# GFNet mixing and a SoLU block on one core: entry 0 stays in one SBUF buffer, and the output weights are converted in steps 0 to 3

## The chip, the cores and the metric

The kernel runs on one core of one Trainium2 chip. A core has five engines with instruction queues of their own: TensorE (PE, matrix products into PSUM), VectorE (DVE), ScalarE (ACT), GpSimd (POOL) and SyncE (SP, which issues DMAs here). Each engine works through its own queue in order; semaphores hold an instruction until what it needs is there. DMAs are issued from the queues of SP, ACT and POOL. The metric is the device time of one execution in microseconds.

## The reference

The first half is a global filter over the sequence, for 8 batch entries of 3136 positions by 256 channels; the second half is a SoLU block over the 25088 rows that come out.

```python
X = np.fft.rfft(x, axis=1)                       # (8, 3136, 256)
Y = X * (filt_r + 1j * filt_i)[None]
y = np.fft.irfft(Y, n=3136, axis=1)              # -> (25088, 256)

h = y @ w_in                                     # 256 -> 1024
sm = softmax(h)                                  # with 1e-9 in the denominator
solu = h * sm
ln = (solu - mean) / np.sqrt(var + 1e-6) * g_ln
out = ln @ w_out                                 # 1024 -> 256
```

The weights w_in and w_out arrive as 8-byte floats; the kernel reads them as pairs of 32-bit words and converts them to fp32 with integer operations on DVE.

## The kernel before, in words

**The transform.** 3136 = 49 x 64. Two ends of the 64 are folded onto each other, so one entry is held as 98 rows (2 x 49) by 32 places by 256 channels. Four products make the filter: *pa* over the 49 (98 rows in, 100 rows out: 25 frequencies s times 4 parts a), *pb* over the 64 (one pair of frequencies at a time, with tables *de*), the product with the filter on DVE (*multiply*: four products of 128x512 and two adds), *pc* back over the 64 (*inverse*), and *py* back over the 49. Between pa and pb the roles of partitions and free places change: pa leaves (s, a) on the partitions and the place m free; pb wants (a, m) on the partitions and s free. The same turn is wanted, the other way, between pc and py. The kernel before makes both turns through DRAM: `store_first` writes pa's result to d1, `fetch` reads it back in the other order; `store` writes pc's result to d2 and `fetch_first_back` reads it.

**The opening** handles entry 0 alone, before anything else can run: its eight pieces of x (four places each) into one tile `rows_x`, pa per piece with a copy by ACT (L240), the trip over d1, seven units of pb, multiply and pc (start, multiply, inverse in one loop; `idle` products keep PE busy in gaps), the trip over d2, and py into y (`back`, L409, copies on ACT at L412). Beside it stand the loads of the filters and tables (`load_tables`, eight filter DMAs and one table each for three groups), the transposes of the tables (`tables_back`, L497), the loads of the weights' words (`begin`) and their conversion (`convert`, `load_float64`): four blocks of w_in and four of w_out, of 128x512 each. Blocks of w_in are multiplied by powers with a negative sign, and use ACT for one product and POOL for another and the add; those of w_out use DVE for all but the add. Blocks 0 and 1 are converted while d1 is written, 2 and 3 while d2 is written and read, the four of w_out beside py and the first products. `weight_sums` makes four differences of w_in blocks for the seven-product scheme below. The remaining jobs of the opening are six pieces of x of entry 1 into free room in y (`fetch_second`, L476) and four stores of the filters in their loaded order to f_dram (L624).

**The steps.** After that, 196 blocks of 128 rows pass through `step(k)`, two blocks (a pair j) per two steps, in an order written out by hand. The products h = y @ w_in of a pair take seven products m1 to m7 of 128x512 on sums of halves (`product`, L759; the sums s on POOL in `pair_sums`), brought together by ACT (`keep`, L769) and DVE (`finish`, L783 and L780, which also keep a running maximum). Then ACT takes the exponential, DVE multiplies (`normalize`, L805), DVE transposes 32x32 blocks (`turn`, L823), SP regroups by DMA (`regroup`, L840), POOL makes sums (L738) and PE multiplies by w_out (`project`, L895) from step LAG = 9 on. So step 9 is the first that needs w_out. `prepare_w_out` makes w_out ready in seven parts, all called at the end of step 0: scale by g_ln (16 operations, L696) and set the ones; the mean over rows on PE (`ps_mean`, L704) with a copy on ACT; four subtractions of the mean (L709); four differences of blocks (L157).

Entry 1's transform runs inside steps 0 to 22 (the table PLAN gives the step of each pa, pb and back), its pa products in steps 0 and 1 (L238), its pb from step 4 on. `early`, `middle`, `late`, `loads`, `first_parts` and so on are lists of such jobs, called at fixed places in `step`. The order inside one engine's queue is the order in which the program issues; nothing is moved at run time.

Of the kernel before, what the change touches and what calls it, by code (L numbers as in the profile page):

```python
# [17 lines left out]
P = 128  # L18
# [34 lines left out]
def dft_tables():  # L53
# [19 lines left out]
    for a, part, sign in ((0, 0, 1), (1, 1, -1), (2, 1, 1), (3, 0, 1)):  # L73
# [19 lines left out]
    return wf.reshape(NR, NK).astype(f32), wq.reshape(P, 2, 64).astype(f32), \  # L93
        wi.reshape(NK, NR).astype(f32), wb.reshape(P, N1).astype(f32), de.astype(f32)
# [3 lines left out]
def kernel(  # L98
# [11 lines left out]
    wf_host, wq_host, wi_host, wb_host, de_host = dft_tables()  # L110
    wf_dram = nc.inline_tensor(wf_host, name="wf_tbl").ap()
    wq_dram = nc.inline_tensor(wq_host, name="wq_tbl").ap()
# [26 lines left out]
    wi_t = consts.tile([NK, NR], FP32, name="wi_t")  # L139
# [56 lines left out]
    class Spectrum:  # L196
# [144 lines left out]
        def inverse(self, i, pss):  # L341
            de, prods = self.des.pop(i), self.prods.pop(i)
            for r in range(2):
                for u in range(self.shape(i)[0]):
                    rows = slice(NQ * u, NQ * u + NQ)
                    self.product(i, pss[u][NQ * r:NQ * r + NQ], lambda v: de[rows, v, 1, r, :],
                                 prods[r][rows])
            self.gs[i] = self.buffer(i, "g", [P, 4, C])
            for u in range(self.shape(i)[0]):
                w = self.shape(i)[1]  # L350
                nc.scalar.copy(out=self.gs[i][:, u:2 * w:2, :], in_=pss[u][:, 0:w, :])
# [6 lines left out]

    def fetch_first_back(ch):
        d = d2[0].rearrange("s (a n) c -> (s a) n c", a=4)  # L360
        for rows in (slice(0, NK - 4), slice(NK - 4, NK)):
            for n in ([0, 1] if ch == 0 else [ch] if ch > 1 else []):
                nc.sync.dma_start(out=t4s[0, n][rows], in_=d[rows, NCH * n:NCH * n + NCH, :])
# [52 lines left out]
    with ExitStack() as st:  # L416
        fpool = pool("fp", 1, stack=st)
        pools = {name: pool(name + "0", bufs, stack=st)
                 for name, bufs in (("r", 1), ("t2", 1), ("p", 2), ("g", 4))}
        wpool = pool("wp", 5, stack=st)  # L420
        ps_h = pool("ps_h", 3, PSUM, stack=st)

        def load_words(src, n):
            raw = wpool.tile([P, 512, 2], I32, name=f"raw_{n}", tag="raw")
            nc.gpsimd.dma_start(
                out=raw.rearrange("p (k d) w -> p k d w", d=src.shape[-2]) if len(src.shape) == 4 else raw,
                in_=src)
            return raw

        def load_float64(dst, raw, negate, share, add=nc.gpsimd.tensor_tensor):  # L430
# [3 lines left out]
            power = wpool.tile([P, 512], I32, name="power", tag="power", bufs=2)  # L434
# [7 lines left out]
            if negate:  # L442
                ts(out=power, in0=power, scalar1=255.0, scalar2=None, op0=ALU.min)
                ts(out=power, in0=power, scalar1=23, scalar2=-2 ** 31, op0=ALU.logical_shift_left,
                   op1=ALU.bitwise_or)
            else:
                ts(out=power, in0=power, scalar1=255.0, scalar2=2.0 ** 23, op0=ALU.min, op1=ALU.mult)
# [7 lines left out]
            if share:  # L455
                nc.scalar.mul(rest, lo, 2.0 ** -44)
                nc.gpsimd.tensor_tensor(out=rest, in0=rest, in1=power.bitcast(FP32), op=ALU.mult)
            else:
                stt(out=rest, in0=lo, scalar=2.0 ** -44, in1=power.bitcast(FP32), op0=ALU.mult,
                    op1=ALU.mult)  # L460
            add(out=dst, in0=dst, in1=rest, op=ALU.add)
# [45 lines left out]
        for h in range(2):  # L507
            for half in range(2):
                weights.append((w_out_sb[:, (0, 6, 1, 2)[2 * h + half]].rearrange("p k d -> p (k d)"),
                                w_out_words[512 * h:512 * h + 512, P * half:P * half + P].rearrange(  # L510
                                    "(k p) d w -> p k d w", p=P)))
# [11 lines left out]
        def begin(j):  # L523
            raws[j] = load_words(weights[j][1], j)
# [4 lines left out]

        rows_x = pools["r"].tile([P, NH, C], FP32, name="x_0", tag="r")  # L530
# [7 lines left out]

        st.enter_context(tc.manual_schedule())
        nc.sync.dma_start(out=wf_t, in_=wf_dram)  # L540
# [4 lines left out]
        fetch_x(0, 0, NH, N1 - 1, 1, nc.sync.dma_start)  # L545
        for i in range(pieces):
            if i:
                fetch_x(0, NCH * i, NCH, 0, N1 - 1, nc.sync.dma_start)
            fetch_x(1, NCH * i, NCH, 0, N1, nc.gpsimd.dma_start)
            if i in (4, 7):  # L550
                begin(i // 7)
        load_tables(0, 4, nc.gpsimd.dma_start)
        load_tables(4, 4, nc.gpsimd.dma_start)
        for i in range(pieces):
            sp.xs[i] = rows_x[:, NCH * i:NCH * i + NCH]

            sp.first(i, (0, 1), ps_h.tile([P, 2, 512], FP32, name=f"pa_0_{i}", tag="h"),
                     nc.scalar.copy, sp.xs[i][0:NK])
            sp.store_first(i, 0, lambda out, in_: by_16((nc.scalar.dma_start, nc.sync.dma_start), out, in_))
# [10 lines left out]
        idle_row(5, "idle")  # L570

        def convert(j):
            load_float64(weights[j][0], raws.pop(j), negate=j < 4, share=j < 4,
                         add=(nc.vector if j == 7 else nc.gpsimd).tensor_tensor)

        for j in range(2):
            convert(j)

        def start(i):
            sp.fetch_filter(i)  # L580
# [5 lines left out]
        sp.fetch(0, nc.sync.dma_start)  # L586
        for i in range(1, units - 2):
            sp.fetch(i, nc.sync.dma_start, spare_piece(i - 1))
            if i == 3:
                load_tables(8, NP - 8, nc.sync.dma_start)  # L590
        for i in range(2):
            start(i)
            tables_back(4 * i, 4)
        for i in range(units):
# [4 lines left out]
            sp.multiply(i, 0, nc.vector.tensor_tensor)  # L599
# [3 lines left out]
            sp.inverse(i, pss)  # L603
            sp.store(i, nc.scalar.dma_start)
            if i == 0:
                nc.gpsimd.dma_start(out=wi_t, in_=wi_dram)
                nc.gpsimd.dma_start(out=wq_t, in_=wq_dram)
                nc.gpsimd.dma_start(out=wb_t[:, 0:N1], in_=wb_dram)
                nc.gpsimd.dma_start(out=g_sb, in_=moe_g_ln.rearrange("(k p) -> p k", p=P))
            elif i == 1:  # L610
                for last_one in (units - 2, units - 1):
                    sp.fetch(last_one, nc.gpsimd.dma_start, spare_piece(last_one - 1))
            for j in {2: (2,), 3: (3, 4), 4: (5,), 5: (6,)}.get(i, ()):
                begin(j)
        idle_row(14, "idler")
        rows_t4 = pools["r"].tile([P, NH, C], FP32, name="t4_0", tag="r")
        for ch in range(pieces):
            t4s[0, ch] = rows_t4[0:NK, NCH * ch:NCH * ch + NCH]
        for ch in range(pieces):
            fetch_first_back(ch)  # L620
# [556 lines left out]
```

## Time and profile before

| | us |
|---|---|
| three runs | 1606.48, 1591.15, 1596.14 |
| median | 1596.14 |
| the profiled execution | 1601.33 |
| its span in the trace | 1599.6 |

| engine | busy us | share of the span |
|---|---|---|
| PE, products | 1551.8 | 97% |
| DVE | 1250.7 | 78% |
| POOL | 1169.7 | 73% |
| ACT | 921.4 | 58% |

The profile is of one execution, with times from the start of its span. A line of the timeline gives the start, the duration, the engine, the line in the kernel, the operation, what it writes and reads, its shape and how many were merged; in brackets stands how long the engine was idle before it and what ended that. "Busy" of PE is modelled from pipelined products, so a busy PE need not be at its peak. The granted clock is that which PE got, as a share of full speed. Some moments of the opening: the first pa starts at 10.6, the first pb at 42.1, the first py at 81.4, the first product of step 0 at 95.7; the DMAs move 267 GB/s on average from 0 to 100 us.

### The profile page before, as it was taken

The page shows a single profiled execution, that of the slowest core. Times are in us where ns is not written, and L with a number is a line of the kernel's source. Part 1 is how long each engine was busy: PE and PEld are TensorE (multiplying, and loading weights), DVE is VectorE, ACT ScalarE, POOL GpSimd, SP SyncE. Part 2 cuts the span into 40 slices and gives each one's busy share as a digit, 9 for nine tenths or more (in the row PEclk, how much of TensorE's full clock was granted, in tenths as well). Part 3 has the DMA queues.
Part 4 walks back from the last instruction along what each step waited for, and adds up shares of the span by engine and source line. Part 5 has one row for each costly group of instructions (what it writes and reads, how often), then busy time and mean ns, then how long its engine had stood idle before and what let it go on. Part 6 is the DMA issues. An engine that isn't in the chain of part 4 may idle for free.

```text
span 1599.6 us, 36769 instructions
## 1 busy us (share of the span) xinstructions
PE 1551.8 (97%) x12828; PEld 1058.8 (66%) x12828; DVE 1250.7 (78%) x2248; ACT 921.4 (58%) x1874; POOL 1169.7 (73%) x1371
## 2 busy tenths in 40 slices
PE   5998999999999999999999999999999999999997
PEld 1463566666666676677666677667766777777777
DVE  1887878897987788876988789887888777777673
ACT  2246555656665656666565655666565656666663
POOL 5546886789677868796779867797766766676765
PEclk8999999999999999999999999999999999999999
DMA  9989878786987589766886679766784444343434
GB/s 266 290 282 269 247 215 236 215 217 181 255 241 222 155 229 256 211 183 178 221 231 202 166 193 251 204 189 179 215 224 132 126 133 122 103 113 94 116 105 116
DMA packets 343802, 311.13 MB, mean 195 GB/s; under 512 B 27834, under 2 KB 310099, under 8 KB 343619
## 3 DMA queue, kind: packets, MB, share of 16 engines
q1 hardware_dynamic: 271476, 170.45, 40.6%
q0 software_dynamic: 33744, 98.81, 21.0%
q10 hardware_dynamic: 38400, 39.53, 8.2%
q8 instruction: 104, 1.70, 0.5%
q14 instruction: 78, 0.64, 0.1%
HBM read 124.51 MB, written 81.40 MB: 129 GB/s over the span
## 4 chain that ended last, share of the span: by engine, by line
PE 84%; DMA 9%; DVE 2%; POOL 1%; issue 1%; SPq 1%; ACT 0%; DVEq 0%; POOLq 0%; ACTq 0%
PE m L759 35%; PE o L895 34%; DMA solu_t<-turn 4%; PE py L386 4%; PE pc L313 3%; PE pb L313 3%; PE pa L281 2%; DMA x<-in_x_dram 2%; DMA f<-in_filt_r_dram 1%; SPq L840 1%; PE idler L563 1%; PE pa L238 1%; PE py L409 1%; DMA out_dram<-ot 1%; POOL u L738 1%
## 5 line engine op out<-in xcount | busy, mean ns | idle before, releaser
L895 PEld LDWEIGHTS o<-w_out_sb,solu_t 128*128 128x128 f32 x3136 | 381.5, 192 | 50.2 <-issue 43.6
L895 PE MATMUL o<-w_out_sb,solu_t 128*128 128x128 f32 x3136 | 400.9, 276 | 3.6 <-DVE ot L915 2.9
L759 PE MATMUL m<-w_in_sb,s 128*128 128x512 f32 x784 | 399.0, 610 | 2.7 <-ACT h L769 1.8
L895 PEld LDWEIGHTS o<-w_out_sb,u 128*128 128x128 f32 x2352 | 307.1, 192 | 138.9 <-issue 106.0
L895 PE MATMUL o<-w_out_sb,u 128*128 128x128 f32 x2352 | 310.6, 275 | 2.5 <-POOL u L738 1.8
L759 PE MATMUL m<-w_in_sb,y 128*128 128x512 f32 x588 | 307.6, 606 | 1.5 <-DVE h L780 1.1
L805 DVE SCALAR_TENSOR_TENSOR h<-e,h 128x1024 f32<-128x1024 f32 x196 | 304.1, 1551 | 0.1
L769 ACT COPY h<-m 128x512 f32<-128x512 f32 x294 | 173.2, 589 | 206.5 <-PE m L759 187.0
L911 ACT ACTIVATE ot<-o,rs_t 128x128 f32<-128x128 f32 x392 | 143.6, 368 | 245.2 <-PE o L895 243.8
L738 POOL TENSOR_TENSOR u<-solu_t 128x512 f32<-128x512 f32 x98 | 135.5, 1383 | 195.6 <-DMA solu_t<-turn 133.6
L783 DVE CUSTOM_DVE_ANT_0 h<-m,h 128x512 f32<-128x512 f32 x196 | 134.2, 685 | 176.8 <-ACT h L769 103.0
L813 ACT ACTIVATE h<-h,nmu 128x1024 f32<-128x1024 f32 x196 | 225.0, 1148 | 52.0 <-DVE turn L823 51.8
L823 DVE STREAM_TRANSPOSE turn<-h 128x1024 f32<-128x1024 f32 x196 | 243.1, 1240 | 3.2
L793 ACT ACTIVATE e<-h,nmax 128x1024 f32<-128x1024 f32 x196 | 225.4, 1150 | 7.9 <-DVE h L805 6.5
L738 POOL TENSOR_TENSOR u<-solu_t,u 128x512 f32<-128x512 f32 x98 | 137.7, 1405 | 95.8 <-PE o L895 95.5
L759 PEld LDWEIGHTS m<-w_in_sb,s 128*128 128x128 f32 x784 | 128.1, 191 | 89.5 <-issue 68.9
L915 DVE SCALAR_TENSOR_TENSOR ot<-o,rs_t,ot 128x128 f32<-128x128 f32 x299 | 103.7, 347 | 98.8 <-ACT ot L911 59.0
L738 POOL TENSOR_TENSOR u<-u,solu_t 128x512 f32<-128x512 f32 x98 | 159.1, 1624 | 15.5 <-PE o L895 6.4
L759 PEld LDWEIGHTS m<-w_in_sb,y 128*128 128x128 f32 x588 | 96.6, 191 | 96.7 <-issue 46.6
L738 POOL TENSOR_TENSOR solu_t<-solu_t,solu_t 128x512 f32<-128x512 f32 x98 | 153.9, 1571 | 0.9
L738 POOL TENSOR_TENSOR s<-y 128x128 f32<-128x128 f32 x196 | 99.8, 509 | 0.5
L386 PEld LDWEIGHTS py<-wb_t,t 50*64 50x64 f32 x3584 | 57.6, 134 | 42.9 <-issue 18.7
(126 smaller groups left out, 1969.1 us busy)
## 6 DMA issues: line engine op xcount, KB each, us to landing
solu_t<-turn SPq DMA_DIRECT2D x780, 128.0 KB
out_dram<-ot SPq DMA_DIRECT2D x196, 128.0 KB
t<-d POOLq DMA_DIRECT2D x112, 200.0 KB, 7.0
d<-x POOLq DMA_DIRECT2D x100, 200.0 KB, 5.3
f<-f_dram POOLq DMA_DIRECT2D x39, 512.0 KB, 8.1
t<-d ACTq DMA_DIRECT2D x37, 512.0 KB
d<-g POOLq DMA_DIRECT2D x36, 512.0 KB, 5.1
x<-in_x_dram SPq DMA_DIRECT2D x112, 98.0 KB
```

The costliest lines, as they stand in the source:

```text
L386: nc.tensor.matmul(out=views[g][64 * h:64 * h + 64, cb, i, :], lhsT=t4[rows, i, c0:c0 + 64], rhs=wb_t[rows, 0:N1], start=True, stop=True)
L738: nc.gpsimd.tensor_tensor(out=out, in0=in0, in1=in1, op=op)
L759: nc.tensor.matmul(out=ms[j, bank], lhsT=lhsT, rhs=w_in_sb[:, w, :], start=m in (1, 2, 7), stop=True, skip_group_check=True)
L769: nc.scalar.copy(out=h_half(k, i), in_=ms[j, 0])
L783: nc.vector.tensor_tensor_reduce(out=h_half(k, i), in0=ms[j, bank], in1=h_half(*kept), scale=1.0, scalar=sofar, op0=ALU.add, op1=ALU.min, ...
L793: nc.scalar.activation(out=e, in_=hs[k], func=AFT.Exp, bias=nmaxs.pop(k)[:, 1:2], scale=-1.0, accum_out=esums[g][:, i:i + 1])
L805: nc.vector.scalar_tensor_tensor(out=solu, in0=e, scalar=SHRINK, in1=solu, op0=ALU.mult, op1=ALU.mult, accum_out=nmu)
L813: nc.scalar.activation(out=solu, in_=solu, func=AFT.Square, bias=nmu, scale=-float(DFF), accum_out=variances[g][:, i:i + 1])
L823: nc.vector.transpose(out=turns[g][:, :, i, :], in_=solus[k].rearrange("p (f j) -> p f j", j=32))
L895: nc.tensor.matmul(out=pos[p, bank], lhsT=lhs[:, f, :], rhs=w[:, f, :], start=f == 0 and (m in (1, 2, 7) or alone), stop=True, skip_group_ ...
L911: nc.scalar.activation(out=out_half(p, *to)[0], in_=pos[p, 0], func=AFT.Copy, scale=rs)
L915: nc.vector.scalar_tensor_tensor(out=ot, in0=pos[p, bank], scalar=rs, in1=out_half(p, *kept)[0], op0=ALU.mult, op1=ALU.add)
```

## The change

Entry 0 no longer goes through DRAM between its products. pa is made 128 rows wide (`wf0`: four groups of 32 partitions, 25 frequencies and zeros in each), and its result goes back into `rows_x`, in place, as (a, s) on the partitions by m by channel. DVE then transposes 32x32 blocks, in place, in four instructions of 64 channels by 32 places each: s and m change places inside each group of 32 partitions. pb reads `rows_x` directly, `inverse` writes its result back into `rows_x`, and after four more such transposes py reads it from there. py now takes all pieces of the first channel half, then all of the second. The stores to and reads from d1 and d2 of entry 0 are gone.

Around it: x's last rows come in four DMAs; the first piece of x's second half is loaded from ACT's queue; tables, filters, w_in's blocks 1 to 3 and the small tables come from SP's queue, and entry 1's x and the filter stores follow there; both adds of the opening's `multiply` are on POOL; `tables_back` for the first two groups comes before pb; 6 idle products stand before pb and 6 before py, where 5 and 14 stood. Only block 0 of w_in is converted ahead of the first turn; 2, 1 and 3 come after the second. The negative sign of the w_in blocks is now in the tables wi and wb, and a conversion is nine DVE operations, with nothing on ACT or POOL.

The four blocks of w_out are loaded (`load_w_out`, SP) after the opening's DMAs into a tile of the steps' own pools, and converted and scaled at the end of steps 0, 1, 2 and 3 (`convert_w_out`: nine operations and four of scaling each). The ones and the mean follow at the end of step 3, the subtractions and differences at the end of step 4. A pool named gap keeps a stretch of SBUF free during the opening.

```diff
+    wf0[:, :, :NS] = wf.reshape(NR, NS, 4).transpose(0, 2, 1)
+    wi0[:, :NS] = wi.reshape(NS, 4, NR).transpose(1, 0, 2)
...
-        def inverse(self, i, pss):
+        def inverse(self, i, pss, out=None):
...
-            self.gs[i] = self.buffer(i, "g", [P, 4, C])
+            self.gs[i] = self.buffer(i, "g", [P, 4, C]) if out is None else out
...
+            stt(out=rest, in0=lo, scalar=2.0 ** -44, in1=power.bitcast(FP32), op0=ALU.mult, op1=ALU.mult)
+            nc.vector.tensor_tensor(out=dst, in0=dst, in1=rest, op=ALU.add)
...
-            fetch_x(1, NCH * i, NCH, 0, N1, nc.gpsimd.dma_start)
-            if i in (4, 7):
-                begin(i // 7)
-        load_tables(0, 4, nc.gpsimd.dma_start)
-        load_tables(4, 4, nc.gpsimd.dma_start)
...
+        fetch_x(1, 0, NCH, 0, N1 - 1, nc.scalar.dma_start)
...
+            fetch_x(1, NCH * i, NCH, 0, N1 - 1, nc.gpsimd.dma_start)
+            if i == 4:
+                begin(0, nc.gpsimd.dma_start)
+        load_tables(0, 4, nc.sync.dma_start)
+        load_tables(4, 4, nc.sync.dma_start)
+        load_tables(8, NP - 8, nc.sync.dma_start)
+        for j in (2, 1, 3):
+            begin(j, nc.sync.dma_start)
...
+        for i in range(pieces - 2):
+            ps = ps_h.tile([P, 2, 512], FP32, name=f"pa_0_{i}", tag="h")
+            for h in range(KD):
+                first_rows(ps, h, i, h)
+            nc.scalar.copy(
+                out=rows_x[:, NCH * i:NCH * i + NCH, :].rearrange("p m (h c) -> p h m c", h=KD),
+                in_=ps.rearrange("p h (m c) -> p h m c", m=NCH))
...
+        def turn_rows(first, size=64):
+            part = rows_x[:, :, first:first + size].rearrange("p m c -> p c m")
+            nc.vector.transpose(out=part, in_=part)
+
+        convert(0)
+        idle_row(3, "idle")
+        tables_back(0, 4)
+        idle_row(3, "idles")
+        tables_back(4, 4)
+        for first in range(0, C, 64):
+            turn_rows(first)
...
-            sp.multiply(i, 0, nc.vector.tensor_tensor)
+            sp.multiply(i, 0, nc.gpsimd.tensor_tensor)
...
-            sp.inverse(i, pss)
-            sp.store(i, nc.scalar.dma_start)
...
+            sp.inverse(i, pss, rows_x[:, 4 * i:4 * i + 4, :])
+        idle_row(6, "idler")
...
+        for first in range(0, C, 64):
+            turn_rows(first)
+        for j in (2, 1, 3):
+            convert(j)
         weight_sums(w_in_sb)
-        for j in (5, 6, 7):
-            convert(j)
-        for ch in range(pieces):
-            for cb in range(KD):
+        for cb in range(KD):
+            for ch in range(pieces):
                 back(0, ch, cb, nc.scalar.copy)
...
+    def convert_w_out(n):
+        i, h, _ = quarters[n]
+        power = pools["p"].tile([P, 512], I32, name=f"power_{n}", tag="pt")
+        load_float64(w_out_sb[:, i].rearrange("p k d -> p (k d)"), raw_out[:, n], power)
+        for f in range(KF // 2):
+            fg = KF // 2 * h + f
+            nc.vector.tensor_scalar(out=w_out_sb[:, i, f], in0=w_out_sb[:, i, f],
+                                    scalar1=g_sb[:, fg:fg + 1], scalar2=-1.0 / SHRINK,
+                                    op0=ALU.mult, op1=ALU.mult)
...
-        if k == 0:
-            for n in range(7):
+        if k < 4:
+            convert_w_out(k)
+        if k == 3:
+            prepare_w_out(0)
+            prepare_w_out(1)
+        if k == 4:
+            for n in range(2, 7):
                 prepare_w_out(n)
...
+        for n in range(4):
+            load_w_out(n, nc.sync.dma_start)
```

## The prediction

> **What bounds the kernel now.** The page comes first: TensorE (PE) is busy 97% of the span and 84% of the chain of waits, so whatever starts PE's dense stretch earlier shortens the run, and work on other engines counts only where PE is not yet dense.
>
> ```profile
> span 1599.6 us, 36769 instructions
> PE 1551.8 (97%) x12828; PEld 1058.8 (66%) x12828; DVE 1250.7 (78%) x2248; ACT 921.4 (58%) x1874; POOL 1169.7 (73%) x1371
> PE   5998999999999999999999999999999999999997
> ```
>
> Next the timeline of the opening, PE's instructions, cut to those that end a stage (start, duration, line, idle before).
>
> ```profile
> 25.75 1.02 PE L238 MATMUL pa<-x,wf_t 98*100 98x512 f32 x2
> 35.23 6.93 PE L563 MATMUL idle<-f,de 128*128 128x512 f32 x10 [8.45 <-DMA f<-in_filt_r_dram]
> ...
> 42.08 1.11 PE L313 MATMUL pb<-t,de 64*64 64x256 f32 x16
> ...
> 81.44 14.43 PE L409 MATMUL py<-wi_t,t 100*128 100x98 f32 x128
> ...
> 95.71 1.93 PE L759 MATMUL m<-w_in_sb,y 128*128 128x512 f32 x4
> ```
>
> Two DRAM trips show: 26.8 to 42.1 (first products to first pb) and 69.9 (last L351 copy) to 81.6 (first py). Step 0 starts at 95.7.
>
> Last, VectorE (DVE) in the same timeline, since the change gives it work: one weight conversion with GpSimd idle, the kernel's only transpose, and the first finish of step 5.
>
> ```profile
> 86.89 0.42 DVE L437 TENSOR_SCALAR raw<-raw 128x512 int32<-128x512 int32 x1
> ...
> 90.28 0.68 DVE L459 SCALAR_TENSOR_TENSOR raw<-raw,power 128x512 f32<-128x512 int32 x1
> 90.88 0.42 DVE L437 TENSOR_SCALAR raw<-raw 128x512 int32<-128x512 int32 x1
> ...
> 103.20 3.15 DVE L696 TENSOR_SCALAR w_out_sb<-w_out_sb,g_sb 128x128 f32<-128x128 f32 x16
> ...
> 126.96 1.24 DVE L823 STREAM_TRANSPOSE turn<-h 128x1024 f32<-128x1024 f32 x1
> ...
> 136.84 0.69 DVE L783 CUSTOM_DVE_ANT_0 h<-m,h 128x512 f32<-128x512 f32 x1 [1.64 <-ACT h L769]
> ```
>
> PE has gaps until about 172 (window 163 to 169: 4.2 of 6 us busy) and is dense after. Between 103 and 172 DVE waits some 20 us in all, in pieces of 0.2 to 4.6 us. So two clocks matter: when PE reaches step 0, and when DVE is through its work of steps 0 to 8.
>
> **The change, part by part.** All times are of the profiled execution (1601.33 us, 5.2 above the median 1596.14); I forecast a difference and add it to the median.
>
> *Loads and first products.* x's second half, first piece, moves from GpSimd's queue (landed at 10.58, 9.2 after its issue) to ScalarE's; the other pieces stay and still pace: GpSimd's later issues show them landing from 12.5 to 24.5. Behind x, SP now issues 27 table and filter DMAs; SP issued such ones every 0.76 to 1.16 us (L484), so they are out by about 40, before pb needs them, and three w_in blocks follow. Bounds: 2 us earlier (PE starts a piece sooner), 5 us later (two queues share what moved 220 GB/s in 10 to 20). Taken: nothing; products end at 26.8. The last two pieces are copied by channel half, so all first-half copies are done at 26.2, the second half's at 27.8. The one conversion left ahead of them needs its words, which landed at 20.7, and 4.6 us: it ends at 25.3.
>
> *First turn.* Four transposes of 128x2048. L823's pitch is 1.16 us for 1024 columns, so 2.25 each and 9.0 in all: 26.2 to 35.2. But L823 reads packed rows of 32; here both sides step 1 KB per element, and no row of this trace does that on DVE. Lower end: L823's pace. Upper end: GpSimd's 128x512 in 1.28 us, 2.5 ns a column, 5.1 each, 20.5 in all. Rows that read PSUM at a stride of 49 elements keep their pace (L399: 392 columns in 0.56 us against 0.69 for 512), and L437 reads every second word at 0.42; both are nearer the lower end, which I take. pb starts at 35.3, 6.8 earlier.
>
> [...]
>
> *Middle.* The back tables' transposes (two L497 rows) leave the path and both adds go to GpSimd: pb to the end of pc 0 takes 1.2 + 4 x 0.61 + 1.28 + 0.8 = 5.7 instead of 7.5. GpSimd's two adds (2.6 a unit) fit in the pitch of 2.9, which PE, ScalarE's copies and the two PSUM buffers set; nothing but these adds stands in its queue. Twenty more us as before: the last copy lands at 61.4 (69.9 before).
>
> *Second turn and py.* py's first channel half needs two turns: 61.4 + 4.5 = 66.0; the other two end at 70.4, before py wants them at 73.2. py takes 14.4: step 0 starts at 80.4 instead of 95.7. **PE gains 15.3 us here.** The six idle products cover 5.2 of that gap, so PE stays warm. 12.8 MB of DRAM traffic goes too (d1 and d2 of entry 0, each written and read: four times 3.2, by the DMA issues of 0 to 100).
>
> *What DVE pays.* Three w_in conversions stand behind the second turn: 8 operations in 3.99 plus an add of 0.61, 4.6 each. In the order on DVE, step 0's finish stands in the middle of the third and waits for m2 (82.6). So: 70.4, 75.0, 79.6, 80.5, wait 2.1, finish 0.7, rest 3.8 (87.1), four differences at 0.61 (89.6). PE is done with m1, m2 and four pa at 85.9 and waits 3.2 for the third of them; before, these were ready long before. Behind that wait stand m6, m7 and all of entry 1's pa: m3, m4 of step 1 end at 100.7.
> Then four output conversions, one at each end of steps 0 to 3, 4.6 + 4 x 0.2 = 5.4 each, instead of beside py (66 to 102). DVE: 89.6 to 95.0; step 1's finishes wait 1.3 and 2.8 for PE, end 101.5; second conversion to 106.9; finish and normalize to 108.8; third to 114.2; step 3's five operations (finish, turn, finish, finish, normalize) to 118.8; fourth to 124.2. m7 of step 2 and m4 of step 3 wait for finishes queued behind conversions. ps_mean stands ahead of step 4's m1 and m2 and needs the fourth: 124.3 + 3.6, m1 and m2 to 129.6, and DVE's next finish waits for that, 5.4 us idle. Then finish, turn, normalize, two products (4.3) and the mean and differences now put here (4.9): **step 5's finish starts at 139.0, against 136.84: 2.2 us late.** The 15.3 us are spent: 21.6 of conversions and 12 of DVE waits stand in front of a step that had that work done.
> Two small terms. PE ends step 3's m4 at 115.9 and idles 8 us before ps_mean; after 8.45 idle it ran at a granted clock of 0.50 to 0.56 from 35.2 to 39.2, so ps_mean may take 2 us more (0 to +2; I take +2). [...] On the other side, x of entry 1, the filter stores (3.2 MB) and the w_out words are off the queues by then: before, waits of 1.27 (t from d1), 0.28 and 2.0 (y from f_dram) stood in steps 4 to 7. 0 to -3.5; I take -2, as solu_t's burst stays. Sum: **+2 us, 1598**. From step 9 on PE is dense and nothing changes.
>
> **Rivals.** *Faster.* DVE's 20 us of waits between 103 and 172 swallow the conversions, and PE keeps its lead: 15.3 less, 1581. For it: those waits are real, and DMA in 130 to 170 is busy 0.9 to 1.0. Against: the conversions stand in order in front of finishes, and 12 us of waits remain between them. Partly right, it gives 1585 to 1592.
> *Slower.* The strided transposes. All eight are on the path (four before pb, four before the conversions), so each us per transpose is 8 us of end: at GpSimd's pace, 5.1 each, +23, 1621. Over 1% (16 us, about what a measurement of this kernel can tell from no change) it decides from 4.0 us per transpose. For it: nothing here strides so. Against: the rows above.
> *Not what it says.* The table DMAs behind x hold GpSimd's x pieces: the first turn starts 5 late and everything behind it: 1603.
>
> **Numbers.** Forecast, +2 give or take 5: 0.48. Faster rival, whole or part: 0.22. Slower rival: 0.18. Late loads: 0.12. Eight in ten: 1582 (leaves out the fullest case of the first rival) to 1617 (turns of up to 4.6 us inside). Faster by over 1% (below 1580) needs the whole lead and more: 0.12. Over 1% slower (above 1612): the strided turns and a late load with a cold PE: 0.20. Within: 0.68.
>
> **What would show it.** In the changed profile: the eight transposes at 2.2 to 2.3 us each (over 4 is the slower rival); pb near 35, py near 66, the first m near 80; conversions of 4.6 with no GpSimd beside them; PE idle before ps_mean and DVE idle after it; step 5's first finish near 139. If that finish is before 130, the faster rival holds; if pb is past 38 with short transposes, loads were late.

## The result, and the profile after

| | before | after |
|---|---|---|
| median of the runs | 1595.18 us (1591.15 to 1606.48) | 1618.24 us (1616.61 to 1621.94) |
| profiled execution, its span | 1601.33, 1599.6 | 1616.61, 1614.8 |
| after / before | | 1.0122, 95% interval 1.0089 to 1.0154 |

The change makes the kernel 1.2% slower. The forecast was 1598, so it was 20 us off, and the median lies just past the upper end of the range (1617). The two medians alone give 1.0145, inside the interval; as a ratio, the upper end of the range is 1617 / 1596.14 = 1.0131. Either way the result stands at that end. What came true is the rival called "slower".

The page of the changed kernel: its span, the busy line, and PE's busy share in 40 slices.

```profile
span 1614.8 us, 36632 instructions
...
PE 1548.7 (96%) x12814; PEld 1063.0 (66%) x12814; DVE 1272.2 (79%) x2256; ACT 918.4 (57%) x1870; POOL 1136.9 (70%) x1335
...
PE   5895899999999999999999999999999999999997
```

PE does 3 us less work than before (1548.7 against 1551.8) in a span that is 15 us longer. The holes are in the first five slices (40 us each), as before, but they are bigger. So the reading goes on in the timeline of the opening: PE first (start, duration, line, idle time before it).

```profile
8.32 13.48 PE L558 MATMUL pa<-x,wf_t 98*128 98x512 f32 x24 [8.32 <-DMA x<-in_x_dram]
21.64 3.60 PE L558 MATMUL pa_last<-x,wf_t 98*128 98x512 f32 x8
...
41.12 4.75 PE L318 MATMUL pb<-x,de 64*64 64x256 f32 x48 [8.95 <-DVE x L591]
...
76.76 17.25 PE L408 MATMUL py<-wi_t,x 128*128 128x98 f32 x128 [3.50 <-issue]
93.85 1.91 PE L767 MATMUL m<-w_in_sb,y 128*128 128x512 f32 x4
...
102.48 3.25 PE L767 MATMUL m<-w_in_sb,s 128*128 128x512 f32 x4 [3.23 <-DVE w_in_sb L162]
...
140.74 5.36 PE L712 MATMUL ps_mean<-w_out_sb,ones 128*128 128x128 f32 x32 [7.76 <-DVE ones L706]
```

The DRAM trips are gone, and yet pb starts at 41.1 (42.1 before) and step 0's first product at 93.9 (95.7 before): of the 15.3 us that PE was to gain, 1.9 are there. The timeline of DVE says what took their place, and what follows from it.

```profile
24.60 16.38 DVE L591 STREAM_TRANSPOSE x<-x 128x2048 f32<-128x2048 f32 x4 [7.17 <-DMA f<-in_filt_r_dram]
...
68.44 16.40 DVE L591 STREAM_TRANSPOSE x<-x 128x2048 f32<-128x2048 f32 x4 [4.49 <-ACT x L356]
...
111.14 0.69 DVE L791 CUSTOM_DVE_ANT_0 h<-m,h 128x512 f32<-128x512 f32 x1 [2.29 <-ACT h L777]
...
114.88 0.75 DVE L788 TENSOR_SCALAR_CACHE_REDUCE h<-m,nmax 128x512 f32<-128x512 f32 x1 [3.04 <-PE m L767]
...
147.96 0.69 DVE L791 CUSTOM_DVE_ANT_0 h<-m,h 128x512 f32<-128x512 f32 x1 [7.28 <-PE m L767]
...
152.06 3.57 DVE L717 TENSOR_TENSOR w_out_sb<-w_out_sb,w_bar 128x512 f32<-128x512 f32 x4
155.55 2.60 DVE L162 TENSOR_TENSOR w_out_sb<-w_out_sb 128x512 f32<-128x512 f32 x4
158.07 0.68 DVE L791 CUSTOM_DVE_ANT_0 h<-m,h 128x512 f32<-128x512 f32 x1
...
194.91 0.35 DVE L923 SCALAR_TENSOR_TENSOR ot<-o,rs_t,ot 128x128 f32<-128x128 f32 x1 [0.51 <-PE o L903]
```

Each set of four transposes takes 16.4 us and not 9.0. Between 102.98 and 140.55 DVE has four output conversions of 5.7 to 6.1 us each (23.6 in all) and waits only 2.3 and 3.0 for others. Then it waits 7.3 for ps_mean and step 4's products, does the mean and the differences in 6.0, and reaches step 5's first finish at 158.07, where the kernel before was at 136.84. All of that delay reaches the first output (L923): 194.91, 21.0 later than in the kernel before, whose DVE timeline has

```profile
173.93 0.35 DVE L915 SCALAR_TENSOR_TENSOR ot<-o,rs_t,ot 128x128 f32<-128x128 f32 x1 [0.75 <-PE o L895]
```

Behind the first output every profiled execution of this study has 1417 to 1426 us left, the changed kernel's 1419.9 and the one of before 1425.7. The one of before is 6 us above its median, and most of that seems to lie there; the changed kernel's is 1.6 below its own. So the spans differ by 15 and the medians by 23. The start of the first output is therefore the yardstick for the experiments.

### The profile page after: what moved, and what is told of

It is laid out like the page before. It is cut to its first block, busy times and chain, and to the rows that moved or that the text cites. A ratio compares the mean times of both kernels' runs of the same rounds, so it can differ in the third digit from the quotient of the medians.

```text
span 1614.8 us, 36632 instructions
## 1 busy us (share of the span) xinstructions
PE 1548.7 (96%) x12814; PEld 1063.0 (66%) x12814; DVE 1272.2 (79%) x2256; ACT 918.4 (57%) x1870; POOL 1136.9 (70%) x1335
## 5 line engine op out<-in xcount | busy, mean ns | idle before, releaser
L813 DVE SCALAR_TENSOR_TENSOR h<-e,h 128x1024 f32<-128x1024 f32 x196 | 296.2, 1511 | 0.0
L923 DVE SCALAR_TENSOR_TENSOR ot<-o,rs_t,ot 128x128 f32<-128x128 f32 x299 | 103.7, 347 | 100.6 <-ACT ot L919 59.1
```

Of the source, the lines that this page charges most:

```text
L813: nc.vector.scalar_tensor_tensor(out=solu, in0=e, scalar=SHRINK, in1=solu, op0=ALU.mult, op1=ALU.mult, accum_out=nmu)
L923: nc.vector.scalar_tensor_tensor(out=ot, in0=pos[p, bank], scalar=rs, in1=out_half(p, *kept)[0], op0=ALU.mult, op1=ALU.add)
```

## The experiments

The theory after this result: **the strided transposes took away the lead that was to pay for the output weights, and the output weights, put on DVE in steps 0 to 4, cost what they were forecast to cost.** The rivals: the transposes alone make the kernel slow and DVE's waits take the conversions in; or the reverse, the transposes don't matter because DVE is late whatever they do.

### The output weights left out, half and whole

The first run leaves the four output conversions and their scaling out; the output weights are a constant. ps_mean, mean and differences stay where the change puts them.

```diff
-        if k < 4:
-            convert_w_out(k)
...
+            nc.gpsimd.memset(w_out_sb[:, i].rearrange("p k d -> p (k d)"), 2.0 ** -6)
```

> The changed kernel with the four output conversions and their scaling left out of steps 0 to 3; the output weights are set to a constant by GpSimd while it idles in the opening, so only these values differ. ps_mean, the mean and the differences stay. Theory (VectorE's order sets the end in steps 0 to 5, so moved conversions are paid almost in full): step 0 starts at 93.9 as in the changed kernel, step 5's first finish falls from 158 to 138 (135 to 141) and the time to 1598. Rival (the strided turns alone make the changed kernel slow, VectorE's waits take the conversions in): finish after 150, time above 1610.

Measured: 1604.86 us, ratio to the kernel before 1.0035 (1.0019 to 1.0051; so with all ratios below). Step 5's first finish is at 146.16, the first output at 183.05. DVE's waits in its timeline:

```profile
110.83 0.69 DVE L793 CUSTOM_DVE_ANT_0 h<-m,h 128x512 f32<-128x512 f32 x1 [8.08 <-ACT h L779]
...
114.57 0.75 DVE L790 TENSOR_SCALAR_CACHE_REDUCE h<-m,nmax 128x512 f32<-128x512 f32 x1 [3.04 <-PE m L769]
...
120.75 0.69 DVE L793 CUSTOM_DVE_ANT_0 h<-m,h 128x512 f32<-128x512 f32 x1 [4.57 <-PE m L769]
...
124.21 0.69 DVE L793 CUSTOM_DVE_ANT_0 h<-m,h 128x512 f32<-128x512 f32 x1 [1.43 <-ACT h L779]
```

The finish is neither at 138 nor past 150; the truth lies between. Without conversions DVE waits 17.1 us in steps 1 to 3 (the four rows). With them 5.7 are left (2.29, 3.04 and 0.36). So 11.4 of the 23.6 us of conversions fit into waits, and the other half is the 11.9 by which the first output of the changed kernel is later (194.91 against 183.05).

The second run leaves the same work out and puts ps_mean, mean and differences back beside step 0.

```diff
-        if k == 3:
-            prepare_w_out(0)
-            prepare_w_out(1)
-        if k == 4:
-            for n in range(2, 7):
+        if k == 0:
+            for n in range(7):
                 prepare_w_out(n)
```

> As the run without output conversions (their values are a constant set by GpSimd, so conversion and scaling are left out), and ps_mean, the mean and the differences back beside step 0, where the kernel before has them: what is left of the change is the opening with its turned rows. Theory (the turns just pay for the DRAM trips they replace, and everything the end lost came with the output weights): step 0 starts at 93, step 5's first finish at 135 to 138, time 1594 to 1599, the same as before within 0.4%. Rival (strided turns and w_in conversions behind them cost on their own): finish after 141, time above 1602.

Measured: 1598.65 us, 1.0015 times the kernel before (0.9998 to 1.0031). Its timelines, first PE and then DVE:

```profile
94.23 1.91 PE L769 MATMUL m<-w_in_sb,y 128*128 128x512 f32 x4
102.86 3.25 PE L769 MATMUL m<-w_in_sb,s 128*128 128x512 f32 x4 [3.23 <-DVE ones L708]
...
105.90 4.16 PE L714 MATMUL ps_mean<-w_out_sb,ones 128*128 128x128 f32 x32
```

```profile
138.73 0.69 DVE L793 CUSTOM_DVE_ANT_0 h<-m,h 128x512 f32<-128x512 f32 x1 [1.41 <-ACT h L779]
...
174.64 0.35 DVE L925 SCALAR_TENSOR_TENSOR ot<-o,rs_t,ot 128x128 f32<-128x128 f32 x1 [0.51 <-PE o L905]
```

The first output is 0.7 later than in the kernel before. The turned rows, with transposes of 4.2 us, just pay for the DRAM trips: neither gain nor loss. This flatters the opening a little, since the kernel before does its four output conversions beside py and this run does none; step 5's first finish is 1.9 later than before, just past the theory's 138. The first rival falls: the transposes alone do not make the kernel slow. The 8.4 between the two runs (183.05 against 174.64) come with ps_mean ahead of step 4's products and the 6 us of mean and differences in front of step 5's finish; the runs do not part these two. Together the output weights cost 20.3 us of first output.

### What a stride costs the transposes

Three kernels put the stride on one side or take it away. A second buffer `rows_t`, channel-major, takes ScalarE's results. Read side or write side or both of the transposes are then packed runs of 32, and what is left of the stride (128 bytes) goes to ScalarE's writes, to TensorE's reads, or to both. To make room, raw words of w_in lie in unused parts of w_out_sb.

```diff
+        rows_t = pool("t0", 1, stack=st).tile([P, C, NH], FP32, name="rows_t", tag="t")
+        by_rows = rows_t.rearrange("p c m -> p m c")
# write side strided: ScalarE writes by_rows, pb and py read rows_x as before
+            nc.vector.transpose(out=part, in_=rows_t[:, first:first + size, :])
# read side strided: ScalarE writes rows_x as before, pb and py read by_rows
+            nc.vector.transpose(out=rows_t[:, first:first + size, :], in_=part)
# packed: ScalarE writes by_rows, pb and py read by_rows
+            part = rows_t[:, first:first + size, :]
+            nc.vector.transpose(out=part, in_=part)
```

> The changed kernel with a second buffer of 32 KB per partition, so that the first products and pc's results are copied by ScalarE straight into channel-major order. The eight transposes then read packed runs of 32 and only their write steps 1 KB. To make room the raw words of w_in blocks 1 to 3 lie in unused parts of w_out_sb, and the pools are in another order. Theory (the step of 1 KB sets the pace, 4.1 us a transpose instead of 2.3 for packed rows): if a stride on each side costs half, 3.2 us a transpose and 7 us off the end (1611); if the write side alone costs, 4.1 us and no gain (1618); if the read side alone costs, 2.3 and 15 us off (1603). Rival (the transposes are slow for another reason, such as their length of 2048 columns): 4.1 whatever the side. ScalarE's copies may cost up to twice as much, up to 4 us on the path.

> As the run before with the other side: the transposes read at a step of 1 KB and write packed runs into the second buffer; pb's products and py's weight loads then read at a step of 128 bytes on TensorE. Theory: the mirror of the run before; 3.2 us a transpose and 7 us off the end if both sides cost the same, and together the two runs' excess over 2.3 must make up the 1.8 measured with both sides strided. Rival: 4.1 here as well as there. TensorE's strided reads may take some of the gain back: py over 17.3 us would show it.

> Both sides of the transposes packed, in place in the second buffer; ScalarE writes and TensorE reads at the step of 128 bytes. Theory: 2.3 us a transpose, eight of them 15 us less on the path; pb at 34, step 0's first product at 79, step 5's first finish at 143 instead of 158, and the time 1603 (1598 to 1608). Rival 1: the moved output conversions on VectorE set the end whatever the turns do, then step 0 starts early but step 5's finish stays after 152 and the time above 1612. Rival 2: the stride is only handed to ScalarE and TensorE, whose copies and products lengthen by what the turns lose; then pb and py are no earlier.

Measured: 1618.11 us, ratio 1.0114 (1.0072 to 1.0156), for the stride on the write side; 1627.02, 1.0170 (1.0128 to 1.0213), on the read side; 1619.77, 1.0124 (1.0076 to 1.0171), packed. The transposes as groups of instructions (count, busy us, mean ns of one), first the changed kernel with both sides strided, then write side, read side, packed:

```profile
L591 DVE STREAM_TRANSPOSE x<-x 128x2048 f32<-128x2048 f32 x8 | 32.8, 4238 | 11.7 <-DMA f<-in_filt_r_dram 7.2 <-ACT x L356 4.5
```

```profile
L596 DVE STREAM_TRANSPOSE x<-rows_t 128x2048 f32<-128x2048 f32 x8 | 28.4, 3654 | 13.3 <-DMA f<-in_filt_r_dram 7.6 <-ACT rows_t L356 5.6
```

```profile
L596 DVE STREAM_TRANSPOSE rows_t<-x 128x2048 f32<-128x2048 f32 x8 | 28.9, 3679 | 9.8 <-DMA f<-in_filt_i_dram 5.3 <-ACT x L356 4.5
```

```profile
L596 DVE STREAM_TRANSPOSE rows_t<-rows_t 128x2048 f32<-128x2048 f32 x8 | 17.8, 2281 | 12.9 <-ACT rows_t L577 7.3 <-ACT rows_t L356 5.6
```

Against packed rows either side alone costs 1.4 us, and both together 1.96: they don't add up. Packed they take 2.28, the pace that the forecast took. So the stride is the cause, not the length of the instruction. But the first outputs hardly came earlier or came later (193.64, 202.84 and 196.77 against 194.91), because the stride was handed on. Rival 2 of the packed run is right in that, though not in its sign: there pb and py start 6.2 and 3.6 us earlier (34.94 and 73.15), and py's length takes it back. ScalarE's copies and PE's py, as groups, in the packed kernel:

```profile
L570 ACT COPY rows_t<-pa 128x1024 f32<-128x1024 f32 x6 | 11.1, 2009 | 8.4 <-PE pa L563 8.4
...
L408 PE MATMUL py<-wi_t,rows_t 128*128 128x98 f32 x128 | 28.2, 404 | 0.0
```

The copies double (1013 ns in the changed kernel), and py, whose weights are read at a step of 128 bytes, takes 28.2 us where it took 17.3 (14.43 in the kernel before). The granted clock doesn't explain that: from 73.2 to 80 it was 1.00 and a product of py took 0.21 us, from 82 to 90 it was 0.50, with PE busy throughout, and one took 0.20. In the kernel before, at 1.00, one took 0.11.

The next two kernels make only the first turn's step short: channels in pairs (8 bytes) and in fours (16 bytes), with ScalarE and TensorE on runs of 2 or 4. The second turn stays as it was, since py takes its weights as one evenly spaced row of channels, and serves for comparison.

```diff
+        rows_t = pool("t0", 1, stack=st).tile([P, C // 2, NH, 2], FP32, name="rows_t", tag="t")
+            part = rows_t[:, first // 2:(first + size) // 2].rearrange("p b m g -> p b g m")
+            nc.vector.transpose(out=part, in_=part)
```

> Only the first turn in another layout: channels in pairs, so that its transposes step 8 bytes on both sides (1 KB before, 128 bytes on one side costs 3.7 us, packed 2.3); ScalarE's copies write and pb's products read runs of 2. The second turn stays as in the changed kernel. [...] Rival (every step but one element costs the same): transposes of 4.2, copies of 2.0, products of 2.2.

> [...]

Measured: 1611.25 us, ratio 1.0072 (1.0050 to 1.0093), at 8 bytes; a single execution of 1614.3 at 16. Second turn and first turn as groups, at 8 bytes and then at 16:

```profile
L603 DVE STREAM_TRANSPOSE x<-x 128x2048 f32<-128x2048 f32 x4 | 16.4, 4176 | 4.3 <-ACT x L359 4.3
L599 DVE STREAM_TRANSPOSE rows_t<-rows_t 128x2048 f32<-128x2048 f32 x4 | 8.9, 2283 | 6.9 <-ACT rows_t L580 6.9
```

```profile
L603 DVE STREAM_TRANSPOSE x<-x 128x2048 f32<-128x2048 f32 x4 | 16.5, 4243 | 4.3 <-ACT x L359 4.3
L599 DVE STREAM_TRANSPOSE rows_t<-rows_t 128x2048 f32<-128x2048 f32 x4 | 15.2, 3969 | 6.2 <-ACT rows_t L580 6.2
```

The rival's 4.2 at 8 bytes was wrong: a step of 8 bytes costs nothing (2283 ns, packed 2281), a step of 16 nearly all (3969, where 1 KB takes 4243). ScalarE's copies took 1047 and 1013 ns (1013 in the changed kernel), so that side is nearly free too. With the first turn 7.5 us shorter, step 5's first finish comes at 147.69 and the first output at 184.33, each over 10 us earlier than in the changed kernel. The 3 beyond the turn have a part that can be seen: PE's wait for the input weights is 1.9 instead of 3.2, and the products after it take 1.95 at full clock instead of 3.25. So the second rival falls too: the first turn's time reaches the end in full. No run shortens the second turn and changes nothing else.

### Part of the change in the kernel before

Here the kernel before gets only the new place of the output weights; its DRAM trips stay.

```diff
-            for j in {2: (2,), 3: (3, 4), 4: (5,), 5: (6,)}.get(i, ()):
+            for j in {2: (2,), 3: (3,)}.get(i, ()):
...
+        if k < 4:
+            convert_w_out(k)
```

> The kernel before with one part of the change alone: the output weights are converted on VectorE in steps 0 to 3 and ps_mean stands ahead of step 4's products, as in the changed kernel; the DRAM trips and everything else of the opening stay. Theory (this part costs nearly all of what an earlier start could win): step 0 starts at 95.7 as before, step 5's first finish goes from 136.8 to 155, and the time is 1613 (1609 to 1618). Rival (VectorE's waits in steps 0 to 8 take the conversions in, so the strided turns alone make the changed kernel slow): finish before 142, time 1594 to 1601.

Measured: 1629.51 us, ratio 1.0192 (1.0148 to 1.0236): worse than the whole change. DVE's timeline, the first operation of the first conversion:

```profile
123.71 0.43 DVE L438 TENSOR_SCALAR raw_out<-raw_out 128x512 int32<-128x512 int32 x1 [22.19 <-DMA raw_out<-in_moe_w_out_dram]
```

The words came 22 us late. Their loads were issued only at 119.8, behind the filter stores of this opening (issued 95.7 to 102.6), in whose source buffers they seem to land. So this run doesn't give the price of the moved conversions. It shows that this part needs the earlier stores of the new opening.

### Ways to get the loss back

Two kernels each take one of DVE's burdens off the changed kernel.

```diff
# conversions of w_in: block 2 among the units' products, block 1 ahead of the second turn
+            for job in ahead_jobs[SPLIT[i]:SPLIT[i + 1]]:
+                job()
...
+        convert(1)
         idle_row(6, "idler")
...
-        for j in (2, 1, 3):
-            convert(j)
+        convert(3)
```

> The changed kernel with the conversion of w_in block 2 dealt out between the products of units 2 to 5 and that of block 1 ahead of the second turn, where VectorE waited 0.5 to 4.5 us for other engines; only block 3 and the differences stay behind the turn. Theory: the second turn starts 0.5 us later at most, VectorE is through the input weights 9 us earlier, PE's wait of 3.2 for them goes, VectorE's first output conversion starts at 97 instead of 103, and step 5's finish comes 5 to 8 earlier: 1611 (1608 to 1614). Rival (the products of the middle are bound by VectorE, so that every operation dealt in lengthens it): the turn starts 4 later or more and the time stays at 1616 to 1620.

Measured: 1618.64 us, ratio 1.0119 (1.0094 to 1.0145): nothing gained. In DVE's timeline the second turn starts at 73.42 (68.44 in the changed kernel):

```profile
73.42 16.36 DVE L602 STREAM_TRANSPOSE x<-x 128x2048 f32<-128x2048 f32 x4
```

The rival holds: no wait is left ahead of the turn, and it comes 5 us later, about as long as one conversion. The operations dealt in make 1.9 of it, by which the last copy ahead of the turn starts later (69.97 against 68.04); three of them took 1.4 to 1.8 us beside GpSimd's adds instead of 0.4 to 0.7. Block 1's conversion, which could begin only at 67.96, makes the rest. So waits of 0.5 to 2.8 us between units were no free room here.

```diff
# ScalarE multiplies, GpSimd multiplies and adds; ps_mean at the end of step 4, mean on GpSimd
+                yield lambda: nc.scalar.mul(rest, lo, 2.0 ** -44)
+                yield lambda: nc.gpsimd.tensor_tensor(out=rest, in0=rest, in1=power.bitcast(FP32), op=ALU.mult)
+                yield lambda: nc.gpsimd.tensor_tensor(out=dst, in0=dst, in1=rest, op=ALU.add)
...
+        for n in {4: (1, 2), 6: (3, 4), 7: (5, 6)}.get(k, ()):
+            prepare_w_out(n)
```

> The changed kernel with the output conversions shared as the input ones were in the kernel before (one multiply on ScalarE, one multiply and the add on GpSimd, each block's scaling one step later), ps_mean at the end of step 4 instead of ahead of its products, the mean's subtraction on GpSimd, the differences in steps 6 and 7. Theory: VectorE saves 5.5 us of operations, 7.3 of waiting for ps_mean and 6 of mean and differences ahead of step 5's finish, less some new waits: finish at 143 (139 to 147), time 1603 (1599 to 1608). Rival (GpSimd and ScalarE take in their own queues what VectorE loses): finish after 152, time above 1612.

Measured: 1614.20 us, ratio 1.0090 (1.0067 to 1.0113). Step 5's first finish comes at 146.99, 11 earlier, at the late end of what the theory gave; but the first output comes at 191.67, only 3.2 earlier. GpSimd's timeline and then DVE's show where part of the 8 us was given back:

```profile
146.03 5.41 POOL L732 TENSOR_TENSOR w_out_sb<-w_out_sb,raw_out 128x512 f32<-128x512 f32 x4 [1.63 <-ACT raw_out L729]
151.39 0.75 POOL L684 DMA_DIRECT2D y<-f_dram  x1
...
152.86 2.17 POOL L341 TENSOR_TENSOR pi<-pi,pt 128x512 f32<-128x512 f32 x1
```

```profile
156.37 0.69 DVE L339 TENSOR_TENSOR y<-pb,y 128x512 f32<-128x512 f32 x1 [2.44 <-DMA y<-f_dram]
```

The mean on GpSimd holds the filter load and pi's add behind it, and DVE waits for the first of them; PE waits 4.79 for the second. The finish is the theory's, the time is the rival's.

### Two versions from what was learned

The first has both turns in pairs, the second one's result copied into rows by ScalarE and GpSimd, the conversions shared, the mean's subtraction behind the loads. The second moves the output weights once more: two conversions at the end of step 0, one each at the ends of steps 1 and 2, the scaling of the last among step 3's finishes, ps_mean at the end of step 3, half of the mean on GpSimd and half on DVE.

```diff
+        def copy_rows(first, copy, size=64):
+            copy(out=rows_x[:, :, first:first + size].rearrange("p m (b g) -> p m b g", g=2),
+                 in_=by_rows[:, :, first // 2:(first + size) // 2])
...
# the second version against the first
-        if 1 <= k < 5:
-            scale_w_out(k - 1)
-        if k < 4:
-            convert_w_out(k)
+        for n in {1: (0, 1), 2: (2,)}.get(k, ()):
+            scale_w_out(n)
+        if k < 3:
+            convert_w_out(*((0, 1), (2,), (3,))[k])
```

> All that the runs pointed to, in one kernel. Both turns in pairs of channels (8 bytes), the second one's result copied into rows by ScalarE (three blocks) and GpSimd (one); the first operations of the three w_in conversions stand in VectorE's wait ahead of the second turn, with a multiply each on ScalarE and a multiply and the add on GpSimd; output conversions shared in the same way, scaling one step later, ps_mean at the end of step 4 behind the loads, subtraction of the mean on GpSimd, differences in steps 6 and 7. Theory: turns of 2.3, pb at 34, py at 68, step 0 at 84.5, no wait of PE for w_in; step 4's first finish at 122 to 128 instead of 148, step 5's at 128 to 134 instead of 158; time 1588 to 1596, faster than or the same as before. Rival (GpSimd's and ScalarE's queues give back in steps 5 to 8 what VectorE gains, as with the shared conversions and late mean): finish of step 5 as early, but time 1598 to 1606.

Measured: 1597.13 us, ratio 1.0001 (0.9984 to 1.0017): the loss is got back, nothing is gained. Step 0's first product is at 83.06, step 4's first finish at 123.79 (131.03 before), step 5's at 132.38 (136.84), and yet the first output at 174.60 (173.93): step 5 gave 5 us back. GpSimd's timeline, then PE's:

```profile
131.43 5.42 POOL L767 TENSOR_TENSOR w_out_sb<-w_out_sb,raw_out 128x512 f32<-128x512 f32 x4 [0.78 <-ACT raw_out L764]
```

```profile
138.13 1.09 PE L321 MATMUL pc<-pi,de 64*64 64x256 f32 x8 [2.43 <-POOL pi L344]
```

The mean on GpSimd holds pi's add, and PE waits 2.4 for that: this much of the 5 the rows show. The finishes are the theory's, and the time lies just past its range (to 1596) and short of the rival's (from 1598).

> The run before with the output weights put where VectorE waited: there 4.2 and 3.0 us stood ahead of step 1's finishes (PE's products of entry 1), and GpSimd's 5.4 us for the mean held pi's add and with it step 5. Now two conversions at the end of step 0, one each at the ends of steps 1 and 2, the last scaling among step 3's finishes, ps_mean at the end of step 3, the mean's subtraction half on GpSimd behind step 3's loads, half on VectorE at the end of step 4. Theory (what is put into these waits is free, what stands from step 4 on is paid): step 4's first finish as before at 124 (122 to 127), step 5's at 128 to 131 instead of 132, the first output written at 168 to 171 instead of 174.6, time 1589 to 1594, 0.3% faster than the kernel before. Rival (PE's own pace with ps_mean among its products sets the end by now): first output at 173 or later, time 1595 to 1600.

Measured: 1595.39 us, ratio 0.9978 (0.9957 to 1.0000). Its DVE timeline has the second turn, step 4's first finish and the first output at

```profile
60.51 8.90 DVE L613 STREAM_TRANSPOSE rows_t<-rows_t 128x2048 f32<-128x2048 f32 x4 [0.84 <-ACT rows_t L362]
...
127.05 0.69 DVE L852 CUSTOM_DVE_ANT_0 h<-m,h 128x512 f32<-128x512 f32 x1 [3.54 <-PE m L828]
...
172.21 0.35 DVE L984 SCALAR_TENSOR_TENSOR ot<-o,rs_t,ot 128x128 f32<-128x128 f32 x1 [0.56 <-PE o L964]
```

This is 1.4% faster than the changed kernel (0.9978 / 1.0122 = 0.986, from two sessions) and 0.2% faster than the kernel before, at the edge of what the runs can tell. Of the lead of 11 that PE has at step 0 (84.50 against 95.71) the first output keeps 1.7. The first output lies between theory (168 to 171) and rival (173 or later), and the time in the rival's range. Step 5's first finish, at 133.43, missed the theory's 131. Ahead of step 4's finish DVE waits 3.5 for PE, whose products stand behind ps_mean there, as the rival has it.

## Why the prediction was right or wrong

**The step that failed is the price of the first turn**, "both are nearer the lower end, which I take": 2.25 us a transpose, where 4.1 to 4.2 were measured. The same price stood in the second turn. How the forecast's chain to step 5's first finish (139.0) and the measured one (158.07) differ, stretch by stretch on DVE:

| stretch | forecast | measured | difference |
|---|---|---|---|
| start of the first turn | 26.2 | 24.6 | -1.6 |
| first turn | 9.0 | 16.4 | +7.4 |
| pb to the last copy | 26.2 | 27.5 | +1.3 |
| second turn | 9.0 | 16.2 | +7.2 |
| input weights, step 0's finish | 19.2 | 18.3 | -0.9 |
| steps 1 to 3 with four conversions | 34.6 | 37.6 | +3.0 |
| wait for ps_mean and step 4's products | 5.4 | 7.3 | +1.9 |
| step 4, mean and differences | 9.4 | 10.1 | +0.7 |

14.6 of the 19 are the transposes. The error was in the choice of neighbours. The rows that spoke for the lower end step 49 elements in PSUM (L399) or 8 bytes in SBUF (L437). The runs show that a step of 8 bytes is free (2.28 us a transpose, as with packed rows) and one of 16 is not (3.97, and 4.24 at 1 KB), so the L437 row said nothing of a step of 1 KB in SBUF. The L399 row reads PSUM, and no run here shows that such a row says anything of SBUF. The upper end, GpSimd's 5.1, was too dear. The middle of the two ends, 3.7, would have given 8 x 1.45 = 11.6 more: 1610.

*The loads and first products.* Taken as nothing; they came earlier (pa from 8.32 instead of 10.58, the last copy done at 26.3), inside the bounds. "Late loads" did not happen.

*The middle and the second turn.* The middle of 26 us was right within 1.3. The two turns that py needs ended at 76.6 and not at 66.0. The six idle products were to keep PE warm, but they ended at 73.3, and py began after 3.5 us of idling: its granted clock was 0.50 from 76.8 to 80.0 and 1.00 from 85 on, and it took 17.25 us instead of 14.43 (at 1.00).

*What DVE pays.* This part held in the main. With PE's lead as it was forecast, the weights were to cost 15.3 + 2.2 = 17.5; the opening alone against the whole change gives 20.3 by the first output. PE's wait for the input weights was 3.2, as forecast, but by errors that offset each other: behind the two turns that py needs, the other two took 8.1 and not 4.4, and py 2.8 more. Each output conversion was 5.7 to 6.1 and not 5.4, and the wait for ps_mean 7.3 instead of 5.4.

*The cold ps_mean.* Forecast +2 at most and taken: 5.36 instead of 3.73, so +1.6. The windows of the changed kernel show the clock (the column after POOL is the granted share of full speed):

```profile
102.50:105.50 3.00, 3.00 (x4) 1.19 (x5) 2.90 (x7) 0.59 (x1) 3.00 (x5) 0.58 0.74 188
...
130.90:133.00 2.10, 2.07 (x2) 0.50 (x2) 1.75 (x3) 0.96 (x1) 0.00 (x0) 0.50 0.19 66
...
140.80:144.00 3.20, 3.20 (x15) 3.20 (x16) 0.00 (x0) 0.00 (x0) 0.00 (x0) 0.51 0.00 0
```

After PE idled 3.2, 3.9 and 7.8 us it ran at 0.50 to 0.58; after 1.9 us, in the kernel with pairs, at 1.00. Inside py of the packed kernel the clock fell from 1.00 to 0.50 without any idling. What was missed is that such a price stood behind each of these waits: the m products after the wait for the input weights took 3.25 instead of 1.95.

*DMA easing* (-2) didn't come: from step 5's first finish to the first output it takes 36.8 us, before 37.1.

*The faster rival* had half its mechanism right: waits do take conversions in, 11.4 of 23.6 us. Beside the lost lead this was not enough. *The slower rival*, put at 0.18, is what happened: it decided from 4.0 us a transpose, and at 4.1 it gave 1613; the rest up to 1618 is in the main the three rows of the table from "steps 1 to 3" on.

## What to carry to other kernels

Price an operation whose access pattern is new by the distance in bytes from one element to the next (a transpose took 2.28 us at 8 bytes, 3.97 at 16 and 4.24 at 1 KB), not by the engine's usual pace: a row with another step is no neighbour, and one of another memory may be none. The stride that was moved to other engines was paid there (ScalarE's copies 2.01 us instead of 1.01, py 28.2 instead of 17.3); look for a layout whose step is short for all of them, as that of pairs is (8 bytes: transposes of 2.28, copies of 1.05). When a change buys time on one engine and spends it on another, test the two parts alone: here the buying was worth nothing and the spending cost 1.1% (1.0122 / 1.0015), and a transfer or a mean moved to a "free" engine came back through that engine's queue (words 22 us late; waits of 2.4 and 4.8 us behind the mean).

## What the runs showed of the hardware

A 128x2048 transpose took 2.28 us with packed rows and with a step of 8 bytes on both sides, 3.65 and 3.68 with the step on one side (1 KB against packed rows), 3.97 at 16 bytes and 4.24 at 1 KB on both sides: the first strided side cost 1.4 us, the second 0.6. ScalarE's copies of 1024 columns took 1.01 us in rows, 1.05 in pairs and 2.01 at a step of 128 bytes. PE's 16 products of pb took 1.1 us in rows and 2.2 at 128 bytes, and a product of py, whose weights were read at 128 bytes, 0.20 to 0.21 at a granted clock of 0.50 as at 1.00, where 0.11 were taken in rows at 1.00. GpSimd copied 2048 columns from pairs into rows in 2.06 us, as fast as ScalarE (2.05), although its 512-column adds took 1.27.
